# A gated linear recurrence with mixture-of-adapters on one core: inputs laid out on the host by place in the chunk, loads per tile, and a written order

## The chip, the cores and the metric

The kernel runs on one core of a Trainium2 chip. The metric is device time in microseconds (us) of one execution. Before the change, three runs took 126.5, 127.96 and 129.17 us; the median is 127.96.

## What is computed

Four sequences (B = 4) of 768 steps with 8 heads of 48 elements pass through a recurrence with a state of 48 x 48 per head, and the result (3072 tokens of 384 elements) through a mixture of 8 low-rank adapters, of which each token uses two. `x` below is the recurrence's result with the heads side by side, K is 2, and `sel` holds the two logits minus their maximum.

```python
for t in range(S):
    cur = np.einsum('bhd,bhe->bhde', u[None] * kt, vt)
    y[:, :, t] = np.einsum('bhd,bhde->bhe', rt, state + cur)
    state = wt[:, :, :, None] * state + np.einsum('bhd,bhe->bhde', kt, vt)
...
logits = x @ w_gate
topk = np.argpartition(-logits, K, axis=1)[:, :K]
...
w = np.exp(sel)
w /= w.sum(-1, keepdims=True) + 1e-09
...
        z = x[mask] @ A[e]
        delta[mask] += w[mask, k, None] * (z @ B[e])
return x + delta
```

## The kernel before, in words

The tokens are cut into 24 tiles of 128 (six per sequence); a tile's 128 tokens lie on the 128 partitions. Tiles are put into groups (of 1, 2 and 3 tiles in the first sequence, of 3 and 3 in the others) for the logarithm of w (`ln`, L475) and for the conversion of v to bf16 (`vcast`, L481), both on ACT.

For each tile t the work is a fixed set of named tasks:

- Decay: `csr` (PE, L488 to L492) sums the logarithms over the tile with triangular matrices into the bank `cs_ps`; `expr` (ACT, L500) takes the exponential into the bank `e_ps`, and `multr` (DVE, L511) multiplies r by it. `csk`, `expk`, `multk` (L495, L505, L516) do the same for k with the same two banks.
- The term with u: `rkk` and `rku` (POOL, L520 and L524) form r k u, `diag` (DVE, L528) sums it per head, `dv` (POOL, L533) multiplies v by the sum.
- Within the tile: `trr` and `trk` (PE, L540 and L545) transpose both products, `trev` (L551 on DVE in odd tiles, L553 on ACT in even ones) copies them out, `amm` (PE, L562) multiplies them, and `aev` (DVE, L568) copies the product out under the triangular mask, as tile `at`.
- State and output: `kv` (PE, L578) adds to the state, `sev` (ACT, L584) copies it; `yin` and `yat` (PE, L596 to L610) sum the parts of the output, `xTev` (ACT, L616) copies it to `xT`.
- Adapters: `lg` (PE, L621) makes the logits. In gates of 6, 6, 6, 3, 1, 1 and 1 tiles, `lgs` (ACT, L632) copies them, `gmax` (DVE, L640 and L643) finds the two largest, and `gsub`, `gexp`, `gmul`, `gden`, `gnorm` make the weights (on POOL and DVE; from tile 18 on DVE alone). `zmm`, `zw`, `zT`, `zTev` (L697 to L720) form the weighted inner product, `dmm` (PE, L726 and L728) multiplies by B and adds x, `oev` (ACT, L734) copies to `res`, and `store` (L738) is issued from ACT's queue.

Inputs are read as they lie in memory. A load (L390) takes one of w, k, r, v of a whole sequence into a tile whose heads are padded from 48 to 64 elements; each 48 elements of one head and one token are a run of 192 bytes in memory. r of the first sequence is loaded in six pieces by chunk (L392). All loads are issued from SP's queue, in the order of the list `LOADS` (L791), together with u, the gate weights, A and B. A comes in as it lies; PE turns it (`turn_A`, L754) between two ACT copies (L747 and `evac_A`, L759).

Ahead of everything, `consts` (L419 to L433) sets up masks and identities, and DVE clears the padded tiles (L428) and two weight tiles (L432, L433).

The order of the instructions on each engine is decided when the kernel is built: `Plan` simulates the tasks with their costs, dependencies and the priorities in `PRIO`, `PRIO_HEAD` and `PRIO_TAIL`, and emits the tasks in order of their simulated start. Each engine then works through its own instructions in that order, and waits on semaphores where it needs another engine's result.

Of the kernel before, what the change touches and what calls it, by code (L numbers as in the profile page):

```python
# [8 lines left out]
F32 = mybir.dt.float32  # L9
# [12 lines left out]
    aev=25.65,  # L22
    amm=-15.27,
    cast_A=-11.66,
    cast_B=0.88,
    cast_wg=-60.35,
    consts=-10.85,
    csk=-0.31,
    csr=-14.17,
    diag=42.56,  # L30
    dmm=2.74,
    dv=81.69,
    evac_A=-13.75,
    expk=-72.58,
    expr=-39.57,
    gden=-20.59,
    gexp=-17.6,
    gmax=-31.21,
    gmul=-9.69,
    gnorm=-40.58,  # L40
    gsub=-13.25,
    kv=-18.83,
    ld_A=-22.88,
    ld_B=26.38,
    ld_k0=-6.66,
    ld_k1=21.95,
    ld_k2=52.4,
    ld_k3=-5.23,
    ld_r0c0=-4.41,
    ld_r0c1=-34.52,  # L50
    ld_r0c2=-23.64,
    ld_r0c3=-29.83,
    ld_r0c4=1.38,
    ld_r0c5=13.41,
    ld_r1=-3.05,
    ld_r2=17.81,
    ld_r3=52.81,
    ld_u=-83.12,
    ld_v0=-6.77,
    ld_v1=29.59,  # L60
    ld_v2=44.69,
    ld_v3=71.64,
    ld_w0=-43.71,
    ld_w1=13.24,
    ld_w2=41.57,
    ld_w3=24.4,
    ld_wg=-15.62,
    lg=42.53,
    lgs=-10.33,
    ln=21.58,  # L70
    multk=5.22,
    multr=-87.78,
    oev=-1.78,
    rkk=101.18,
    rku=63.0,
    sev=13.54,
    store=-95.56,
    trev=-30.73,
    trk=-25.52,
    trr=-5.99,  # L80
    turn_A=-2.64,
    vcast=110.5,
    xTev=3.03,
    yat=-18.65,
    yin=23.89,
    zT=-24.79,
    zTev=-5.29,
    zmm=26.3,
    zw=-7.91,
# [5 lines left out]
    aev=-16.79,  # L95
    amm=48.01,
    cast_A=7.5,
    cast_B=-14.13,
    cast_wg=21.27,
    consts=-2.5,  # L100
    csk=-21.41,
    csr=-7.4,
    diag=-4.31,
    dmm=17.09,
    dv=38.59,
    evac_A=10.38,
    expk=11.86,
    expr=-16.57,
    gden=-38.35,
    gexp=-14.3,  # L110
    gmax=4.34,
    gmul=-3.71,
    gnorm=-5.33,
    gsub=-43.86,
    kv=12.49,
    ld_A=-5.03,
    ld_B=12.8,
    ld_k0=-34.63,
    ld_k1=6.6,
    ld_k2=-14.77,  # L120
    ld_k3=11.25,
    ld_r0c0=-24.58,
    ld_r0c1=4.07,
    ld_r0c2=15.4,
    ld_r0c3=6.19,
    ld_r0c4=5.17,
    ld_r0c5=-7.65,
    ld_r1=21.36,
    ld_r2=23.52,
    ld_r3=22.62,  # L130
    ld_u=19.76,
    ld_v0=-12.19,
    ld_v1=1.39,
    ld_v2=0.87,
    ld_v3=-20.68,
    ld_w0=8.25,
    ld_w1=-10.57,
    ld_w2=-9.52,
    ld_w3=26.72,
    ld_wg=5.58,  # L140
    lg=4.13,
    lgs=8.09,
    ln=-22.66,
    multk=10.55,
    multr=-21.15,
    oev=14.15,
    rkk=39.57,
    rku=9.98,
    sev=-2.01,
    store=-13.3,  # L150
    trev=22.53,
    trk=31.94,
    trr=6.82,
    turn_A=22.18,
    vcast=-15.78,
    xTev=-6.57,
    yat=-4.27,
    yin=16.18,
    zT=27.26,
    zTev=33.7,  # L160
    zmm=-3.4,
    zw=17.47,
)
PRIO_TAIL = dict(
    aev=-0.28,
    amm=14.03,
    cast_A=-36.85,
    cast_B=19.87,
    cast_wg=11.74,
    consts=-26.49,  # L170
    csk=9.67,
    csr=25.89,
    diag=34.43,
    dmm=6.24,
    dv=-17.71,
    evac_A=8.83,
    expk=-0.72,
    expr=-40.51,
    gden=23.76,
    gexp=18.47,  # L180
    gmax=-30.09,
    gmul=40.84,
    gnorm=18.15,
    gsub=14.82,
    kv=19.73,
    ld_A=-8.96,
    ld_B=-1.13,
    ld_k0=17.68,
    ld_k1=14.83,
    ld_k2=27.67,  # L190
    ld_k3=-8.08,
    ld_r0c0=32.73,
    ld_r0c1=19.97,
    ld_r0c2=-39.7,
    ld_r0c3=29.48,
    ld_r0c4=-20.14,
    ld_r0c5=6.09,
    ld_r1=-4.78,
    ld_r2=-19.27,
    ld_r3=-29.09,  # L200
    ld_u=40.14,
    ld_v0=3.86,
    ld_v1=-4.67,
    ld_v2=-39.21,
    ld_v3=8.49,
    ld_w0=-33.47,
    ld_w1=-3.25,
    ld_w2=39.94,
    ld_w3=6.14,
    ld_wg=8.51,  # L210
    lg=2.86,
    lgs=42.9,
    ln=-1.58,
    multk=19.03,
    multr=21.62,
    oev=-2.62,
    rkk=37.33,
    rku=-39.38,
    sev=4.33,
    store=0.15,  # L220
    trev=-11.58,
    trk=-3.46,
    trr=26.52,
    turn_A=24.22,
    vcast=-21.25,
    xTev=-23.74,
    yat=1.12,
    yin=21.1,
    zT=-2.43,
    zTev=-1.87,  # L230
    zmm=1.73,
    zw=5.22,
)


class Plan:


    HOP = 0.061
    WAIT = 0.047  # L240
# [5 lines left out]
    def add(self, name, eng, cost, base, deps, fn, far=False, take=None, free=None, lat=0.0, dma=0.0):  # L246
        assert name not in self.tasks, name
        op = name if name in PRIO else name.rstrip("0123456789")
        zone = 1 if base < 3 else 2 if base >= 20 else 0
        prio = base + PRIO.get(op, 0.0) + (PRIO_HEAD if zone == 1 else PRIO_TAIL if zone == 2 else {}).get(op, 0.0)  # L250
        self.tasks[name] = dict(name=name, eng=eng, cost=cost, base=base, prio=prio, deps=deps, fn=fn,
                                far=far, take=take, free=free, lat=lat or dict(DVE=.09, ACT=.1, PE=.17, POOL=.05).get(eng, 0.0), dma=dma, i=self.seq, zone=zone)
        self.seq += 1

    def run(self):
        T = self.tasks
        users, left = {n: [] for n in T}, {}
# [11 lines left out]
        def enter(x):  # L269
            e = x["eng"]  # L270
            rdy = 0.0
            for d in x["deps"]:
                rdy = max(rdy, end_of[d] if T[d]["eng"] == e and not x["far"] else done[d] + self.HOP)
            x["rdy"] = rdy
            ready[e].append(x)
# [50 lines left out]
def kernel(  # L326
    ctx: ExitStack,
    tc: tile.TileContext,
    r: bass.AP,
    k: bass.AP,  # L330
    v: bass.AP,
    w: bass.AP,
    u: bass.AP,
    moe_w_gate: bass.AP,
    moe_A: bass.AP,
    moe_B: bass.AP,
# [3 lines left out]
    B, H, S, D = r.shape  # L340
    L = 128
    NC = S // L
    HD = H * D
    NT = B * NC
    P = H // 2
    E = moe_w_gate.shape[1]
    R = moe_A.shape[2]
    ER = E * R
    DP = 64
# [24 lines left out]
    SRC = dict(r=r, k=k, v=v, w=w)  # L374
    seqs = {}

    def seq_tile(b, key):
        d = seqs.setdefault(b, {})
        if key in "rk":
            if "rk" not in d:  # L380
                d["rk"] = ld.tile([L, 2, H * NC, DP], F32, name="rk")
                d["r"], d["k"] = d["rk"][:, 0], d["rk"][:, 1]
        elif key not in d:
            d[key] = ld.tile([L, H * NC, DP], F32, name=key + "_in", bufs=3 if key == "v" else 2)
        return d[key]

    def load(b, key, c):
        dst = seq_tile(b, key)
        if c is None:
            nc.sync.dma_start(out=dst[:, :, 0:D], in_=SRC[key][b].rearrange("h (c p) d -> p (h c) d", p=L))  # L390
        else:
            nc.sync.dma_start(out=dst.rearrange("p (h c) d -> p h c d", c=NC)[:, :, c, 0:D],  # L392
                              in_=SRC[key][b, :, c * L:(c + 1) * L, :].rearrange("h p d -> p h d"))

# [10 lines left out]
    wg_f = const.tile([128, P, E], F32, name="wg_f")  # L405
    A_f = const.tile([E * H, D * R], F32, name="A_f")
    A_nat = const.tile([E * H, DP, R], BF16, name="A_nat")
    B_f = const.tile([ER, HD], F32, name="B_f")
# [10 lines left out]
    def consts():  # L419
# [7 lines left out]
        for t_ in rk2s[:2] + v_bfs[:2] + dvs[:2] + S_sbs + rk2s[2:] + dvs[2:] + v_bfs[2:]:  # L427
            nc.vector.memset(t_, 0.0)  # L428
# [3 lines left out]
        nc.vector.memset(wg_f, 0.0)  # L432
        nc.vector.memset(A_nat, 0.0)  # L433

    def load_u():
        nc.sync.dma_start(out=u_sb, in_=u.partition_broadcast(128))

    def load_wg():
        for g in range(2):
            nc.sync.dma_start(  # L440
                out=wg_f[g * 64:g * 64 + D],
                in_=moe_w_gate.rearrange("(p g d) e -> g d p e", g=2, d=D)[g])

    def load_A():
        nc.sync.dma_start(out=A_f, in_=moe_A.rearrange("e (h d) r -> (e h) (d r)", h=H))

    def load_B():
        nc.sync.dma_start(out=B_f, in_=moe_B.rearrange("e r d -> (e r) d"))  # L448
# [14 lines left out]
    def chunk(t, key):  # L463
        b, c = divmod(t, NC)
        return seqs[b][key].rearrange("p (h c) d -> p h c d", c=NC)[:, :, c, 0:D]

    def chunks(gi, key):
        g = groups[gi]
        x = seqs[g["b"]][key].rearrange("p (h c) d -> p c h d", c=NC)
        return x[:, g["c0"]:g["c0"] + g["n"], :, 0:D]  # L470

    def ln(gi):
        g = groups[gi]
        lw = wk.tile([L, GN, H, D], FP16, name="logw", bufs=3)
        nc.scalar.activation(out=lw[:, 0:g["n"]], in_=chunks(gi, "w"), func=ACT.Ln)  # L475
        g["logw"] = lw
# [158 lines left out]
    def gmax(q):  # L635
# [3 lines left out]
        for i in range(n):  # L639
            nc.vector.max(out=top[:, i, :], in_=x[:, i, :])  # L640
# [300 lines left out]
```

## Time and profile before

| quantity | value |
|---|---|
| median of three runs | 127.96 us (126.5 to 129.17) |
| the profiled execution's own time | 126.82 us |
| its span, first to last instruction | 125.1 us |
| mean granted clock of TensorE | 0.963 |
| bytes read, written | 19.48 MB, 4.72 MB |
| memory clears of padded tiles on DVE, first start to last end | 2.16 to 9.00 us |
| first logarithm (ACT) starts | 13.31 us |
| first and last masked copy `at` (DVE) start | 21.24 and 113.89 us |
| issue to landing, median, of a whole-sequence load of w, k, v | 10.3, 10.4, 11.2 us |
| issue to landing, median, of a store of 192 KB | 1.9 us |

The profile is of one execution. Engines: PE is TensorE's matmuls, PEld its weight loads, DVE is VectorE, ACT ScalarE, POOL GpSimd, SP the engine that issues the loads; SPq and ACTq are those engines' queues, where DMAs are issued. A line such as "L568 DVE" is an instruction of line 568 of the kernel before. The busy rows cut the span into 40 slices, with one digit of tenths for each. A row of the timeline gives start, duration, engine, line, operation, output and inputs with their shapes, how many instructions were merged, and in brackets how long the engine had been idle and what ended that.

### The profile page before, as it was taken

The page shows a single profiled execution, that of the slowest core. Times are in us where ns is not written, and L with a number is a line of the kernel's source. Part 1 is how long each engine was busy: PE and PEld are TensorE (multiplying, and loading weights), DVE is VectorE, ACT ScalarE, POOL GpSimd, SP SyncE. Part 2 cuts the span into 40 slices and gives each one's busy share as a digit, 9 for nine tenths or more (in the row PEclk, how much of TensorE's full clock was granted, in tenths as well). Part 3 has the DMA queues.
Part 4 walks back from the last instruction along what each step waited for, and adds up shares of the span by engine and source line. Part 5 has one row for each costly group of instructions (what it writes and reads, how often), then busy time and mean ns, then how long its engine had stood idle before and what let it go on. Part 6 is the DMA issues. An engine that isn't in the chain of part 4 may idle for free.

```text
span 125.1 us, 3598 instructions
## 1 busy us (share of the span) xinstructions
PE 94.4 (75%) x1432; PEld 66.3 (53%) x1432; DVE 91.9 (73%) x208; ACT 82.6 (66%) x165; POOL 70.6 (56%) x93
## 2 busy tenths in 40 slices
PE   1000399699789496899994599979998999999840
PEld 0000066456557363577673477667675667877520
DVE  5982153576499598999748577977789999989830
ACT  4000783576985468998850979769998886955550
POOL 6000191588493399999379798812069999900000
PEclk9999999999999958999999959999999999999996
DMA  2879996496899799798889959994950321305063
GB/s 49 251 222 291 215 220 190 86 267 168 205 261 284 198 287 291 200 295 218 231 246 277 266 165 259 275 286 122 314 204 0 128 71 63 129 2 189 5 251 126
DMA packets 33776, 24.42 MB, mean 195 GB/s; under 512 B 7328, under 2 KB 33696, under 8 KB 33760
## 3 DMA queue, kind: packets, MB, share of 16 engines
q1 hardware_dynamic: 30304, 19.48, 57.2%
q10 hardware_dynamic: 3456, 4.72, 10.3%
q8 instruction: 11, 0.18, 0.6%
q14 instruction: 5, 0.04, 0.1%
HBM read 19.48 MB, written 4.72 MB: 193 GB/s over the span
## 4 chain that ended last, share of the span: by engine, by line
SPq 36%; DMA 17%; PE 14%; DVE 12%; ACT 9%; issue 5%; POOL 3%; ACTq 1%; DVEq 0%; POOLq 0%
SPq L390 22%; DMA v_in<-in_v_dram 12%; SPq L392 8%; DMA rk<-in_r_dram 5%; DVE at L568 4%; SPq L448 4%; ACT res L734 2%; SPq L440 2%; ACT e_ps L505 2%; DVE rk L511 2%; POOL rku L524 2%; ACT xT L616 2%; POOL rku L520 2%; PE y_ps L596 1%; PE y_ps L610 1%
## 5 line engine op out<-in xcount | busy, mean ns | idle before, releaser
L520 POOL TENSOR_TENSOR rku<-rk 128x384 f32<-128x384 f32 x24 | 24.1, 1004 | 24.7 <-DMA rk<-in_r_dram 21.1
L568 DVE TENSOR_TENSOR at<-a_ps,at_mask 128x1024 bf16<-128x1024 f32 x24 | 29.2, 1217 | 3.3 <-PE a_ps L562 3.1
L533 POOL TENSOR_TENSOR dv<-v_in,diag 128x384 bf16<-128x384 f32 x24 | 19.6, 830 | 10.3 <-DVE diag L528 4.6
L524 POOL TENSOR_TENSOR rku<-rku,u_sb 128x384 f32<-128x384 f32 x24 | 24.0, 999 | 1.6
L511 DVE TENSOR_TENSOR rk<-rk,e_ps 128x384 bf16<-128x384 f32 x24 | 13.1, 547 | 10.5 <-DMA rk<-in_r_dram 7.7
L492 PE MATMUL cs_ps<-logw,strict 128*128 128x384 f16 x24 | 9.0, 374 | 11.9 <-ACT logw L475 11.9
L516 DVE TENSOR_TENSOR rk<-rk,e_ps 128x384 bf16<-128x384 f32 x24 | 13.1, 546 | 5.5 <-ACT e_ps L505 3.8
L475 ACT ACTIVATE logw<-w_in 128x1152 f16<-128x1152 f32 (+2 forms) x9 | 9.4, 1058 | 11.5 <-DMA w_in<-in_w_dram 11.2
L616 ACT CAST xT<-y_ps 128x512 bf16<-128x512 f32 x24 | 14.1, 588 | 3.3 <-PE y_ps L610 3.2
L500 ACT ACTIVATE e_ps<-cs_ps 128x384 f32<-128x384 f32 x24 | 11.5, 478 | 6.8 <-DVE rk L516 3.2
L528 DVE TENSOR_REDUCE diag<-rku 128x8 f32<-128x384 f32 x24 | 12.9, 546 | 2.9 <-POOL rku L524 2.8
L481 ACT CAST v_bf<-v_in 128x1152 bf16<-128x1152 f32 (+2 forms) x9 | 9.3, 1045 | 7.0 <-DMA v_in<-in_v_dram 7.0
L505 ACT ACTIVATE e_ps<-cs_ps 128x384 f32<-128x384 f32 x24 | 11.6, 484 | 3.2 <-PE y_ps L610 1.4
L545 PE MATMUL trp<-ident,rk 128*128 128x128 bf16 x96 | 10.5, 238 | 3.2 <-DVE rk L516 3.2
L734 ACT COPY res<-d_ps 128x384 f32<-128x384 f32 x22 | 10.6, 483 | 2.9 <-PE d_ps L728 1.5
L553 ACT COPY rkT<-trp 128x1024 bf16<-128x1024 bf16 x12 | 12.2, 1014 | 0.4 <-PE trp L545 0.4
L562 PE MATMUL a_ps<-rkT 48*128 48x128 bf16 x192 | 10.2, 229 | 2.2 <-ACT rkT L553 1.3
L540 PE MATMUL trp<-ident,rk 128*128 128x128 bf16 x96 | 10.5, 239 | 1.2 <-ACT rkT L553 0.5
L610 PE MATMUL y_ps<-at,v_bf 128*64 128x128 bf16 x192 | 10.6, 236 | 0.4 <-DVE at L568 0.4
L601 PE MATMUL y_ps<-ident,dv 128*128 128x128 bf16 x96 | 10.0, 229 | 0.0
L551 DVE COPY rkT<-trp 128x1024 bf16<-128x1024 bf16 x12 | 8.2, 684 | 2.1 <-PE trp L545 2.1
L540 PEld LDWEIGHTS <-rk 128*128 128x128 bf16 x96 | 6.9, 106 | 5.1 <-issue 1.9
(74 smaller groups left out, 176.4 us busy)
## 6 DMA issues: line engine op xcount, KB each, us to landing
out_dram<-res ACTq DMA_DIRECT2D x24, 192.0 KB, 1.9
rk<-in_r_dram SPq DMA_DIRECT2D x6, 192.0 KB, 3.5
u_sb<-in_u_dram SPq DMA_DIRECT2D x1, 192.0 KB, 3.7
A_f<-in_moe_A_dram SPq DMA_DIRECT2D x1, 192.0 KB, 4.2
B_f<-in_moe_B_dram SPq DMA_DIRECT2D x1, 192.0 KB, 6.4
rk<-in_k_dram SPq DMA_DIRECT2D x4, 0.2 KB, 10.4
w_in<-in_w_dram SPq DMA_DIRECT2D x4, 0.2 KB, 10.3
v_in<-in_v_dram SPq DMA_DIRECT2D x4, 0.2 KB, 11.2
```

The source lines that it names most:

```text
L390: nc.sync.dma_start(out=dst[:, :, 0:D], in_=SRC[key][b].rearrange("h (c p) d -> p (h c) d", p=L))
L505: nc.scalar.activation(out=e, in_=cs_ps[:, 0:HD].rearrange("p (h d) -> p h d", d=D), func=ACT.Exp, scale=-1.0)
L511: nc.vector.tensor_mul(rk2[:, 0].rearrange("s p h d -> s (p h) d")[:, :, 0:D], chunk(t, "r"), st[t]["er"])
L516: nc.vector.tensor_mul(rk2[:, 1].rearrange("s p h d -> s (p h) d")[:, :, 0:D], chunk(t, "k"), st[t]["ek"])
L520: nc.gpsimd.tensor_mul(rku, chunk(t, "r"), chunk(t, "k"))
L524: nc.gpsimd.tensor_mul(st[t]["rku"], st[t]["rku"], u_sb)
L528: nc.vector.tensor_reduce(out=dg, in_=st[t]["rku"], axis=AX.X, op=ALU.add)
L533: nc.gpsimd.tensor_mul(dv_[:, :, 0:D], chunk(t, "v"), st[t]["diag"].to_broadcast([L, H, D]))
L540: nc.tensor.transpose(trp[:, 0, p, :], st[t]["rk2"][:, 0, p, :, :].rearrange("s a b -> s (a b)"), ident)
L568: nc.vector.tensor_mul(at, st[t]["a_ps"].rearrange("s g p f -> s (g p) f"), at_mask.to_broadcast([128, H, 128]))
L616: nc.scalar.copy(out=xT_, in_=st[t]["y_ps"])
L734: nc.scalar.copy(out=res, in_=st[t]["d_ps"])
```

## The change

The host puts the inputs into the order in which the kernel uses them: partition first, then tile, head, element (`lay_out`), so that each partition reads one run. r and k of one tile stand side by side in one array; u is repeated for all partitions; the gate weights, A (already turned and padded) and B are one array of 128 rows.

- Loads: one for w and one for v of each group (9 each), one for r and k of each tile (24), one for u, one for the adapter weights: 44, all from SP, into tiles without pad. Buffers: 3 for w, 4 for v, 8 for r and k; `logw` has 4 instead of 3.
- The constants: only the pad columns of the padded work tiles are cleared, and `turn_A`, `evac_A` and the two clears of weight tiles are gone. The three casts read the one weight tile.
- Stores are issued from SP instead of ACT, in the same queue as the loads.
- Gates: the selection `gsel` becomes a task apart from `gmax`. Where a gate has one tile (21, 22, 23), `gnorm` is gone: `zw` multiplies by the weights and by the reciprocal at once. From tile 18 the logits are read from PSUM without `lgs`.
- For tiles 18 to 23, `dx` adds x into the result bank ahead of `dmm`, which then is a single matmul.
- The order is a list of all tasks, `ORDER`, instead of the planner's result. The planner's code is changed too but not used.

Core of the diff:

```diff
+ORDER = """
+consts ld_w0 ld_rk0 ln0 csr0 ld_v0 expr0 rkk0 ld_w1 csk0 multr0 vcast0 expk0 trr0 ld_u multk0 ln1 ld_rk1 kv0 rku0
+csr1 trk0 sev0 expr1 ld_rk2 rkk1 trev0 csk1 multr1 diag0 ld_v1 expk1 amm0 csr2 trr1 multk1 rku1 dv0 rkk2 trk1 aev0
+ld_w2 expr2 vcast1 yin0 csk2 multr2 trev1 rku2 expk2 kv1 yat0 ld_rk3 ln2 diag1 amm1 trr2 csr3 diag2 multk2 dv1
...
+ln3 ld_rk7 rkk6 amm4 diag5 multk5 yat3 cast_A csr6 ld_rk8 aev4 xTev3 lg0 trk5 expr6 yin4 rku6 rkk7 dv5 cast_B ld_v3
...
+expk13 ld_w7 vcast6 csr14 multk13 yat11 zTev3 diag15 expr14 amm12 multr14 store2 ld_rk18 dmm3 trk13 csk14 xTev11
...
+xTev14 expk17 sev16 aev15 trev16 ld_v8 lg14 yin15 csr18 multk17 yat15 amm16 rku19 rku20 zTev6 expr18 diag18 dmm6
+xTev15 multr18 store0 oev6 aev16 csk18 trr17 trk17 expk18 rkk21 rku21 dv18 yin16 store1 ld_rk23 vcast8 trev17 csr19
...
+gden5 zmm22 zT21 dmm19 oev18 zmm23 gexp6 zw22 gsel6 zTev21 dx20 oev19 dmm20 gmul6 store18 gden6 zT22 oev20 dx21 zw23
+dmm21 store19 zTev22 zT23 dx22 oev21 dmm22 zTev23 store20 dx23 dmm23 oev22 store21 oev23 store22 store23
+"""
...
-            nc.sync.dma_start(out=dst[:, :, 0:D], in_=SRC[key][b].rearrange("h (c p) d -> p (h c) d", p=L))
...
+    def load_w(gi):
+        g = groups[gi]
+        g["w"] = ld.tile([L, GN, H, D], F32, name="w_in", bufs=3)
+        nc.sync.dma_start(out=g["w"][:, 0:g["n"]], in_=w[:, g["t0"]:g["t0"] + g["n"]])
+
+    def load_v(gi):
+        g = groups[gi]
+        g["v"] = ld.tile([L, GN, H, D], F32, name="v_in", bufs=4)
+        nc.sync.dma_start(out=g["v"][:, 0:g["n"]], in_=v[:, g["t0"]:g["t0"] + g["n"]])
+
+    def load_rk(t):
+        st[t]["rk"] = ld.tile([L, 2, H, D], F32, name="rk_in", bufs=NRKI)
+        nc.sync.dma_start(out=st[t]["rk"], in_=rk[:, t])
...
-        for t_ in rk2s[:2] + v_bfs[:2] + dvs[:2] + S_sbs + rk2s[2:] + dvs[2:] + v_bfs[2:]:
-            nc.vector.memset(t_, 0.0)
+        pads = [t_.rearrange("s a p h d -> s (a p h) d") for t_ in rk2s]
+        pads += [t_.rearrange("s c h d -> s (c h) d") for t_ in v_bfs] + dvs + S_sbs
+        for t_ in pads:
+            nc.vector.memset(t_[:, :, D:DP], 0.0)
...
+        if alone(q):
+            nc.vector.scalar_tensor_tensor(
+                out=zw_[:, 0], in0=st[t0]["z_ps"][:, 0].rearrange("p (e r) -> p e r", r=R),
+                scalar=gst[q]["den"][:, 0, :], in1=gst[q]["gs"].rearrange("p o e -> p e o").to_broadcast([L, E, R]),
+                op0=ALU.mult, op1=ALU.mult)
+            return
...
-    def dmm(t):
+    def dx(t):
         d_ps = bank(dbank(t), [L, HD], F32, "d_ps")
-        nc.tensor.matmul(d_ps, lhsT=st[t]["zT"], rhs=B_bf, start=True, stop=False, skip_group_check=True)
         for p in range(P):
             nc.tensor.matmul(d_ps[:, p * 2 * D:(p + 1) * 2 * D], lhsT=st[t]["xT"][:, p, :], rhs=ipad,
-                             start=False, stop=(p == P - 1), skip_group_check=True)
+                             start=(p == 0), stop=False, skip_group_check=True)
         st[t]["d_ps"] = d_ps
+
+    def dmm(t):
+        if not own_bank(t):
+            dx(t)
+        nc.tensor.matmul(st[t]["d_ps"], lhsT=st[t]["zT"], rhs=B_bf, start=False, stop=True, skip_group_check=True)
...
-        nc.scalar.dma_start(out=out[t * 128:(t + 1) * 128, :], in_=st[t]["res"])
+        nc.sync.dma_start(out=out[t * 128:(t + 1) * 128, :], in_=st[t]["res"])
...
-    NXT, NRES = 12, 8
+    NXT, NRES, NRKI = 12, 8, 8
...
+    def tok(x):
+        return x.reshape(B, H, S // L, L, D).transpose(3, 0, 2, 1, 4).reshape(L, B * S // L, H, D)
...
+    return dict(
+        w=tok(w), rk=np.stack([tok(r), tok(k)], axis=2), v=tok(v), u=np.broadcast_to(u, (L, H, D)),
+        moe=np.concatenate([rows(moe_w_gate), rows(moe_A.transpose(1, 0, 2).reshape(H * D, E * R)),
+                            moe_B.reshape(E * R, H * D)], axis=1))
```

## The prediction

> **What bounds the kernel now.** I read the page's busy shares and slices first, then the DMA queues, the waits, and the windows and timeline of single stages.
>
> ```profile
> PE 94.4 (75%) x1432; PEld 66.3 (53%) x1432; DVE 91.9 (73%) x208; ACT 82.6 (66%) x165; POOL 70.6 (56%) x93
> PE   1000399699789496899994599979998999999840
> ...
> DMA  2879996496899799798889959994950321305063
> ...
> q1 hardware_dynamic: 30304, 19.48, 57.2%
> q10 hardware_dynamic: 3456, 4.72, 10.3%
> ...
> SPq 36%; DMA 17%; PE 14%; DVE 12%; ACT 9%; issue 5%; POOL 3%; ACTq 1%; DVEq 0%; POOLq 0%
> ```
>
> No engine is full over the span. The slices show two stages: the DMA engines are about nine tenths busy up to slice 29 (91 us), while PE is full only from there. The chain is 36% SP queue and 17% DMA: loads set the pace. Loads (q1) used 0.572 x 16 x 125.1 = 1145 engine-us for 19.48 MB, 58.8 per MB; stores (q10), rows of 1536 B, 206 for 4.72 MB, 43.7 per MB.
>
> ```profile
> POOL rku L520 <- DMA rk<-in_r_dram: 21.1, 5, 12.3
> ACT logw L475 <- DMA w_in<-in_w_dram: 11.2, 1, 11.2
> DVE rk L511 <- DMA rk<-in_r_dram: 7.7, 3, 5.0
> ACT v_bf L481 <- DMA v_in<-in_v_dram: 7.0, 3, 3.4
> ```
>
> These waits (total, count, longest) show the first w arriving 11.2 us after ACT was ready, and later sequences starving the engines again.
>
> ```profile
> 13.31 1.26 ACT L475 ACTIVATE logw<-w_in 128x384 f16<-128x384 f32 x2 [11.24 <-DMA w_in<-in_w_dram]
> 15.12 0.56 DVE L511 TENSOR_TENSOR rk<-rk,e_ps 128x384 bf16<-128x384 f32 x1 [4.99 <-DMA rk<-in_r_dram]
> 21.24 1.23 DVE L568 TENSOR_TENSOR at<-a_ps,at_mask 128x1024 bf16<-128x1024 f32 x1 [1.38 <-PE a_ps L562]
> 96.64 1.22 DVE L568 TENSOR_TENSOR at<-a_ps,at_mask 128x1024 bf16<-128x1024 f32 x1
> 113.89 1.22 DVE L568 TENSOR_TENSOR at<-a_ps,at_mask 128x1024 bf16<-128x1024 f32 x1
> 91.00:114.00 23.00, 22.26 (x386) 16.52 (x384) 22.06 (x55) 18.18 (x43) 17.19 (x21) 1.00 0.23 85
> ```
>
> Each tile has one masked copy of `at` (L568), so its start marks the tile. The first is at 21.24, the last (tile 23) at 113.89: 92.65 / 23 = 4.03 us per tile. From tile 18 (96.64) to 23, with all loads landed, it is 17.25 / 5 = 3.45. The window row gives busy time of PE, PEld, DVE, ACT, POOL: PE 22.26 and DVE 22.06 of 23 us, so compute bounds there. The end after the last `at` is 125.1 - 113.89 = 11.2. Three parts then: head 21.2, 23 intervals, tail 11.2.
>
> **Head.** Loads become one run per partition of 1536 to 4608 B, and w of tile 0 alone comes first, 192 KB. Landing, issue to data: 1.9 us for a 192 KB store, 3.7 for the 192 KB u load with others beside it. Issue at 0.8 gives 2.7 to 4.5; I take 3.4, between the two and nearer the store, since w is first in the queue. From the start of the log (13.31) to the end of the first exponential (14.48 + 0.47) is 1.64, so multr could start at 5.1. Its r and k (384 KB) are next: at 43.7 to 58.8 engine-us per MB (2.7 to 3.7 us per MB on 16 engines) they land 1.1 to 1.5 us after w, in time.
>
> DVE's own start also counts: it clears padded tiles until 10.1. Now only the pad columns are cleared. A memset of 512 words took 485 ns, of 128 words 165: 0.83 ns per word and 58 fixed. The 15 pad memsets cost 2.2 us if done in words, 3.6 if in 2-byte elements, against 6.2 before; wg_f and A_nat (0.57) go. DVE starts these at 2.16 and is free at 5.3 to 6.7; I take 6.0 for multr of tile 0.
>
> Multr to `at` took 21.24 - 15.12 = 6.1. Of that amm waited 1.5 for the A transposition on PE (2.11 us) and the work queued behind it, which the host now does: 4.6 is left (multr 0.56, expk 0.47, multk 0.56, trk 0.63, trev 1.0, amm 0.65, hops). First `at`: 10.6 (9.9 to 11.3). cast_A with its 512 elements costs what evac_A did (0.59 of ACT), later, beside PE's work.
>
> **Middle.** Bytes per tile: 19.48 / 24 = 0.81 MB, 2.2 us at the stores' price, 3.0 at the old loads' price. Both are under 3.45, so after the head DMA should run ahead, up to the eight rk buffers. In list order 3.54 MB stand up to rk of tile 3; at the old price of 3.7 us per MB it lands at 2.8 + 13.0 = 15.8, and its multr wants it at 6.0 + 3 x 3.45 = 16.4: little slack there, a microsecond or two of risk.
>
> The per-tile price has ends 3.3 (100 to 110 us, where PE ran 181 of its 1432 matmuls, 3.03 tiles) and 4.03 (the whole of before, starved). I take 3.6: 3.45, nearest because its loads were there, plus 0.15 for clock dips: twice in the middle the granted clock falls to 0.5 for 3.4 us, 2 x 1.7 / 23. 23 x 3.6 = 82.8.
>
> One rule bears on the dips: the Trainium skill, TensorE: Matmul & The Clock Gate, Part 1, says that the clock is halved after an idle window of about 3.4 us and released by activity. The first dip follows PE waits of 0.65 and 1.03 us at 41 to 43, when loads were late, so the trace does not show a whole idle window. By the rule a fed PE would have no dip, and the sum would be 3.4 lower.
>
> Other edits here: the 24 stores leave ACT (0.34 each, 8.2 us of its issue time, mostly under running ACT work) and go to SP behind loads. SP issues 44 loads and 24 stores. At 0.39 (u) to 0.82 (the first k) that is 27 to 56 us of queue time, beside compute, against issues blocked for 4 to 6 us each now. Store 0 is put behind the loads of v8; its buffer is wanted by oev8 only, eight tiles later, so I price it at nothing; if the cover fails, oev8 waits, and dmm9 behind it for the bank. Reads without pad cost nothing new: POOL took 1004 ns with pad (L520), 999 without (L524). The order list replaces the planner's; no row shows its quality, and 3.3 to 4.03 bounds it.
>
> A rule that speaks against the change: the Trainium skill, DMA: Bandwidth & Descriptors, Rules for kernel authors, asks for 1 MiB or more per DMA for full bandwidth; these are 0.19 to 0.58 MB. Its anatomy of the GpSimd path puts some 2.0 us of fixed cost on each, and if 44 loads paid that in series, my estimate from that page is 88 us of latency and no gain. The last stores show otherwise: they are issued 0.95 us apart while each takes 1.9 to land, so they overlap.
>
> **Tail.** The last rows of ACT are copies of `res` 0.95 apart, 0.48 of work and 0.47 behind a store's issue.
>
> ```profile
> 120.78 0.48 ACT L734 COPY res<-d_ps 128x384 f32<-128x384 f32 x1 [0.47 <-ACT res L734]
> 121.29 0.34 ACTq L738 DMA_DIRECT2D out_dram<-res  x1
> 121.72 0.48 ACT L734 COPY res<-d_ps 128x384 f32<-128x384 f32 x1 [0.47 <-ACT res L734]
> ```
>
> With stores on SP the last copy follows its own matmul (ends 120.9) instead of ACT's queue: -0.7. The last gate loses the normalisation (0.27 from 119.20 to 119.47) and the logit copy (0.17 and a hop), though the fused product may cost up to 0.17 more than the 0.28 of the plain one: -0.4. dx ahead of time takes 0.33 of matmul off the last result: -0.3. 11.2 - 1.4 = 9.8; bounds 9.3 and 11.2.
>
> **Sum.** 10.6 + 82.8 + 9.8 = 103.2 of span. The profiled execution took 126.82 for a span of 125.1, 1.7 around it: 104.9, say 105. That execution lies 0.9% under the median shown, 127.96; I leave 105.
>
> **Rivals.** *Loads still pace it.* If runs of a few KB gain nothing, or waits in SP's list make loads late, the rate stays 4.03: 10.6 + 92.7 + 9.8 + 1.7 = 114.8. For: DMA was nine tenths busy; against: 43.7 against 58.8 per MB, and prefetch eight tiles deep. *Better than fed before.* The list packs all engines at 3.3 and DVE is free early: 9.9 + 75.9 + 9.3 + 1.7 = 96.8. Against: in 91 to 114 PE had 0.7 us idle, little to win. *Slower than before.* SP works strictly in order, so a load whose buffer is late holds all loads behind it; place: ld_rk9 on, each waiting for tile t-8. Price: were each tile's landing of 1.9 us bare, 105 + 23 x 1.9 = 148.7. It decides from 1.0 us bare per tile (128 - 105 = 23). Against: ld_rk8 stands in the list beside tile 4's work, four tiles ahead. *No change*, 125 to 130, needs the same loss at about 1.0 per tile; nothing speaks for it.
>
> **How the numbers follow.** Forecast 0.69; loads pacing 0.15; better 0.08; slower 0.05; no change 0.03. Faster by over 2% (about what a measurement of this kernel can tell from no change) takes the first three: 0.92; within 2%: 0.03; slower: 0.05. The range reaches from the better case, 97, to the pacing case, 115; beyond it lie the 0.08 and some of both ends.
>
> **What would show it.** First log near 3.4, first multr near 6, first `at` near 10.6; `at` spacing 3.4 to 3.7 with PE nine tenths busy; no wait on rk or w above 2 us after the head; queue 1 near 44 engine-us per MB; last `at` near 93.4 and 9.8 after it. Wrong if `at` spacing is near 4 with POOL or DVE waiting on rk, if PE's clock stays at 0.5 for long, or if engines wait on each other in turn with DMA idle: then the list is at fault.

## The result and the profile after

The kernel after takes 103.27 us (median of four runs, 102.98 to 103.59), against 127.23 for the kernel before on the same chip. The ratio is 0.820, with a 95% interval of 0.812 to 0.829. Ratios, here and below, leave out executions more than 1.5% slower than the fastest of the same kernel, so they are not quite the quotients of the medians. The profiled execution took 103.02 us for a span of 101.3. The forecast was 105 with a range of 97 to 115.

The page of the kernel after, in the rows that were shown of before (busy shares; tenths in 40 slices for PE and the DMA engines; the DMA queue; the chain that ended last, by engine):

```profile
PE 85.6 (84%) x1400; PEld 60.7 (60%) x1400; DVE 85.2 (84%) x203; ACT 80.5 (79%) x160; POOL 69.8 (69%) x93
PE   1238899998698699999999999999988999999930
...
DMA  2899999999999976948006989961224003224173
...
q1 hardware_dynamic: 9792, 24.27, 64.5%
...
PE 54%; DVE 22%; ACT 7%; DMA 5%; issue 4%; POOL 3%; SPq 1%; ACTq 1%; DVEq 0%
```

From slice 4 on, PE is now at eight tenths or more in nearly every slice; before, it kept falling to four to seven tenths up to slice 27. The SP queue has gone from the chain, 36% to 1%, and DMA from 17% to 5%. DMA is full or nearly so from slice 2 to slice 14 (35 us), while it runs ahead of the engines, and then has gaps: it no longer sets the pace. Loads and stores now stand in one queue, 0.645 x 16 x 101.3 = 1045 engine-us for 24.27 MB, 43.1 per MB; before it was 58.8 for the loads.

The waits of the kernel after that end on a load (total, count, longest):

```profile
POOL rku L422 <- DMA u_sb<-in_u_dram: 2.6, 1, 2.6
...
POOL rku L418 <- DMA rk_in<-in_rk_dram: 1.7, 1, 1.7
...
ACT v_bf L379 <- DMA v_in<-in_v_dram: 1.6, 1, 1.6
...
ACT logw L373 <- DMA w_in<-in_w_dram: 1.2, 1, 1.2
```

Each occurs once, and all in the first 8.2 us. The first logarithm waits 1.2 us instead of 11.2. From there on no engine waits for a load.

The timeline of the kernel after, its head and the first and last masked copy (start, duration, engine, line):

```profile
3.27 0.52 ACT L373 ACTIVATE logw<-w_in 128x384 f16<-128x384 f32 x1 [1.19 <-DMA w_in<-in_w_dram]
4.87 0.55 DVE L409 TENSOR_TENSOR rk<-rk_in,e_ps 128x384 bf16<-128x384 f32 x1 [0.51 <-ACT e_ps L398]
6.40 0.51 ACT L379 CAST v_bf<-v_in 128x384 bf16<-128x384 f32 x1 [1.56 <-DMA v_in<-in_v_dram]
6.82 0.47 ACT L403 ACTIVATE e_ps<-cs_ps 128x384 f32<-128x384 f32 x1
9.56 1.01 ACT L451 COPY rkT<-trp 128x1024 bf16<-128x1024 bf16 x1
11.46 1.22 DVE L466 TENSOR_TENSOR at<-a_ps,at_mask 128x1024 bf16<-128x1024 f32 x1
91.06 1.22 DVE L466 TENSOR_TENSOR at<-a_ps,at_mask 128x1024 bf16<-128x1024 f32 x1
```

In three parts, profiled execution against profiled execution:

| part | before | after | forecast |
|---|---|---|---|
| head, to the first `at` | 21.24 | 11.46 | 10.6 |
| middle, 23 intervals | 92.65 (4.03 each) | 79.60 (3.46 each) | 82.8 (3.60 each) |
| tail, after the last `at` starts | 11.2 | 10.24 | 9.8 |
| span | 125.1 | 101.3 | 103.2 |

More than half of the gain, 13.0 us, comes from the middle, 9.8 from the head, 1.0 from the tail.

### The profile page after: what moved, and what is told of

The parts are those of the page before. It is cut to its first block, busy times and chain, and to the rows that moved or that the text cites. A ratio compares the mean times of both kernels' runs of the same rounds, so it can differ in the third digit from the quotient of the medians.

```text
span 101.3 us, 3568 instructions
## 1 busy us (share of the span) xinstructions
PE 85.6 (84%) x1400; PEld 60.7 (60%) x1400; DVE 85.2 (84%) x203; ACT 80.5 (79%) x160; POOL 69.8 (69%) x93
## 3 DMA queue, kind: packets, MB, share of 16 engines
q1 hardware_dynamic: 9792, 24.27, 64.5%
HBM read 19.55 MB, written 4.72 MB: 240 GB/s over the span
## 4 chain that ended last, share of the span: by engine, by line
PE 54%; DVE 22%; ACT 7%; DMA 5%; issue 4%; POOL 3%; SPq 1%; ACTq 1%; DVEq 0%
DVE at L466 8%; PE y_ps L508 6%; PE a_ps L460 6%; PE y_ps L499 5%; PE y_ps L494 5%; DMA v_in<-in_v_dram 5%; PE trp L438 4%; PE z_ps L601 4%; PE d_ps L640 4%; PE trp L443 3%; DVE rk L414 3%; DVE rkT L449 3%; PE s_ps L476 3%; PE cs_ps L388 3%; PE s_ps L519 3%
## 5 line engine op out<-in xcount | busy, mean ns | idle before, releaser
L418 POOL TENSOR_TENSOR rku<-rk_in 128x384 f32<-128x384 f32 x24 | 23.9, 998 | 1.7 <-DMA rk_in<-in_rk_dram 1.7
L409 DVE TENSOR_TENSOR rk<-rk_in,e_ps 128x384 bf16<-128x384 f32 x24 | 13.2, 548 | 2.9 <-ACT e_ps L398 2.9
L414 DVE TENSOR_TENSOR rk<-rk_in,e_ps 128x384 bf16<-128x384 f32 x24 | 13.2, 549 | 2.6 <-ACT e_ps L403 2.5
L651 ACT COPY res<-d_ps 128x384 f32<-128x384 f32 x22 | 10.6, 486 | 2.6 <-PE d_ps L647 2.1
L438 PE MATMUL trp<-ident,rk 128*128 128x128 bf16 x96 | 9.8, 227 | 1.0 <-DVE rkT L449 0.7
L390 PE MATMUL cs_ps<-logw,strict 128*128 128x384 f16 x24 | 8.4, 349 | 2.1 <-ACT logw L373 2.1
L508 PE MATMUL y_ps<-at,v_bf 128*64 128x128 bf16 x192 | 9.8, 224 | 0.2
L443 PE MATMUL trp<-ident,rk 128*128 128x128 bf16 x96 | 9.8, 227 | 0.1
L393 PE MATMUL cs_ps<-logw,ident 128*128 128x384 f16 x24 | 8.3, 348 | 0.7 <-ACT e_ps L398 0.6
```

The source lines that it names most:

```text
L409: nc.vector.tensor_mul(rk2[:, 0].rearrange("s p h d -> s (p h) d")[:, :, 0:D], chunk(t, "r"), st[t]["er"])
L414: nc.vector.tensor_mul(rk2[:, 1].rearrange("s p h d -> s (p h) d")[:, :, 0:D], chunk(t, "k"), st[t]["ek"])
L418: nc.gpsimd.tensor_mul(rku, chunk(t, "r"), chunk(t, "k"))
L438: nc.tensor.transpose(trp[:, 0, p, :], st[t]["rk2"][:, 0, p, :, :].rearrange("s a b -> s (a b)"), ident)
L443: nc.tensor.transpose(st[t]["trp"][:, 1, p, :], st[t]["rk2"][:, 1, p, :, :].rearrange("s a b -> s (a b)"), ident)
L508: nc.tensor.matmul(y_ps[g * 64:(g + 1) * 64, p, :], lhsT=vb[:, 2 * p + g, :], rhs=at[:, g * P + p, :], start=False, stop=(p == P - 1), ski ...
```

## The experiments

All times are medians. The ratio is to the kernel before, measured together with each kernel; its medians lay between 125.9 and 128.7. The kernels came in three groups on three chips (runs of 192 bytes, whole sequences, planner, full clears; then stores from ACT and less work on PE, DVE, POOL; then the rest), and the kernel after was not measured again with them, so I read nothing into differences below 0.7 us from it. Parts such as head, spacing and tail are read from one profiled execution of each kernel. Theory at the outset: the loads had set the pace; long runs made them cheap, an early small first load brought the first tile forward, and what is left is bound by compute, PE first.

**Run length alone undone.**

```diff
-        nc.sync.dma_start(out=st[t]["rk"], in_=rk[:, t])
+        nc.sync.dma_start(out=st[t]["rk"].rearrange("p x h d -> p (x h) d"), in_=rk[t].rearrange("x h p d -> p (x h) d"))
...
-        return x.reshape(B, H, S // L, L, D).transpose(3, 0, 2, 1, 4).reshape(L, B * S // L, H, D)
+        return x.reshape(B, H, S // L, L, D).transpose(0, 2, 1, 3, 4).reshape(B * S // L, H, L, D)
...
```

(w and v in the same way.)

> Undoes the run length alone: the host still lays inputs out by tile, in the order of use, but head by head, so that each load reads runs of 192 bytes; loads, buffers and order stay. Theory (the gain is the early first tile and the loads' order; the middle is bound by compute at 3.45 us per tile): loads cost 58.8 engine-us per MB again, which is 3.0 us per tile and still under 3.45, so 104 to 108, first at masked copy at 12 to 13. Rival (the run length itself is what fed the engines): loads pace the middle as before, 4.0 us per tile, 114 or more.

Measured: 133.23 us, ratio 1.036 (1.031 to 1.041): slower than the kernel before. The theory's number fell, and the rival's 4.0 us per tile was not far enough out. The page, two waits and three masked copies (the first, the seventh, the last) of this kernel:

```profile
DMA packets 102737, 24.50 MB, mean 186 GB/s; under 512 B 99392, under 2 KB 102592, under 8 KB 102720
...
q1 hardware_dynamic: 102720, 24.27, 90.7%
```

```profile
POOL rku L418 <- DMA rk_in<-in_rk_dram: 25.2, 10, 4.3
ACT v_bf L379 <- DMA v_in<-in_v_dram: 16.0, 8, 4.9
```

```profile
12.53 1.22 DVE L466 TENSOR_TENSOR at<-a_ps,at_mask 128x1024 bf16<-128x1024 f32 x1
42.55 1.22 DVE L466 TENSOR_TENSOR at<-a_ps,at_mask 128x1024 bf16<-128x1024 f32 x1 [0.26 <-PE a_ps L460]
120.95 1.21 DVE L466 TENSOR_TENSOR at<-a_ps,at_mask 128x1024 bf16<-128x1024 f32 x1
```

The head is nearly that of the kernel after (12.5 against 11.5), but the spacing is (120.95 - 12.53) / 23 = 4.71, and POOL waits ten times for r and k. The reason is the first line. The kernel before read the same runs of 192 bytes, but its page counts 33,776 packets in all, 7,328 of them under 512 B; here there are 102,737, of which 99,392 are under 512 B. A load of a whole sequence went out mostly in packets between 512 B and 2 KB, a load of one to three tiles in packets of one run each; what makes the difference was not isolated. So the old price did not come back, a worse one did: 0.907 x 16 x 131.6 = 1910 engine-us; without the stores (206 in the kernel before) an estimated 1704 for 19.55 MB, 87 per MB. That is 4.4 us per tile, more than the 3.46 of compute. Small loads need the long runs.

**Load size alone undone.** The long runs stay, but each of w, v and r with k comes for a whole sequence.

```diff
-        nc.sync.dma_start(out=st[t]["rk"], in_=rk[:, t])
+        if t % NC == 0:
+            whole["rk"] = ld.tile([L, NC, 2, H, D], F32, name="rk_in", bufs=2)
+            nc.sync.dma_start(out=whole["rk"], in_=rk[:, t:t + NC])
+        st[t]["rk"] = whole["rk"][:, t % NC]
...
```

> Undoes the size alone: long runs as after, but w, v and r with k are each loaded for a whole sequence (1.1 and 2.3 MB) where the list has the first piece. Theory (the first tile waits for its bytes): w lands near 6, r and k near 12.5, so the first multr at 13 instead of 4.9; the middle keeps 3.45; about 110. Rival (large DMAs move faster, and the size of a load costs nothing): 102 to 104.

Measured: 112.22 us, ratio 0.872 (0.867 to 0.877). The theory holds in the main (about 110 was expected), and so do its parts:

```profile
19.40 1.22 DVE L476 TENSOR_TENSOR at<-a_ps,at_mask 128x1024 bf16<-128x1024 f32 x1
98.97 1.22 DVE L476 TENSOR_TENSOR at<-a_ps,at_mask 128x1024 bf16<-128x1024 f32 x1
```

The first log starts at 6.04 and the first multr at 11.65 (6 and 13 expected); ACT then waits for v until 14.34, which the theory had left out. The first `at` is 7.9 us later than in the kernel after, the spacing is the same 3.46, and the end is 8.3 later. Large loads are not faster either: from 3 to 25 us this kernel moved 427 GB/s, the kernel after 415 from 10 to 30, both with all DMA engines full.

**The list taken away.**

```diff
-ORDER = """
-consts ld_w0 ld_rk0 ln0 csr0 ld_v0 expr0 rkk0 ld_w1 csk0 multr0 vcast0 expk0 trr0 ld_u multk0 ln1 ld_rk1 kv0 rku0
...
-"""
+ORDER = ""
```

> Takes the list away: the planner orders the tasks by its costs and the priorities of the kernel after; loads keep their order. Theory (feeding the engines is the change; any sane order gives 3.45): 102 to 106. Rival (the list holds a good part of the gain): 108 or more.

Measured: 160.23 us; its executions spread from 153 to 161, so no ratio is given. The theory falls: an order is not just any order. The first `at` comes at 9.46, earlier than in the list, but the spacing is 5.15, and 30.9 us follow the last `at` instead of 10.2. DMA is idle for most of the second half, so this is not a load. POOL waits 18.9 us for `diag`, ACT 17.9 for PE's outputs. From 115 us on the granted clock is 0.54 on average, so a part of the loss is PE at half speed. It shows that order can cost over 50 us with the same work and loads, but not what the list is worth against the order of the kernel before, since the planner ran here with other costs and priorities.

**The layout alone, in the kernel before.** This gives the missing corner: long runs, whole-sequence loads, the old planner's order, clears and store queue.

```diff
-            nc.sync.dma_start(out=dst[:, :, 0:D], in_=SRC[key][b].rearrange("h (c p) d -> p (h c) d", p=L))
+            nc.sync.dma_start(out=dst, in_=SRC[key][b].rearrange("p c h d -> p (c h) d"))
...
+        inputs[name] = x.reshape(x.shape[0], x.shape[1], -1, 128, x.shape[3]).transpose(0, 3, 2, 1, 4)
```

> Makes the layout alone in the kernel before: r, k, v, w by place in the chunk, tiles without pad, so that whole-sequence loads are one run per partition and the pieces of r 1536 bytes each; number, size and order of the loads, the planner, stores from ACT and clears stay. Theory (the run length fed the engines, the rest is the head): spacing 3.4 to 3.6 instead of 4.03, first masked copy 14 to 17, 107 to 113. Rival (the old order, which the planner made for slow loads, keeps the engines apart when fed): 116 or more.

Measured: 116.63 us (115.77 to 118.73), ratio 0.938 (0.916 to 0.960): at the edge of the rival's range, and outside the theory's. The profiled execution took 117.49:

```profile
19.45 1.22 DVE L565 TENSOR_TENSOR at<-a_ps,at_mask 128x1024 bf16<-128x1024 f32 x1 [1.28 <-PE a_ps L559]
104.54 1.22 DVE L565 TENSOR_TENSOR at<-a_ps,at_mask 128x1024 bf16<-128x1024 f32 x1
```

Read beside the whole-sequence kernel, this splits the gain in three, by profiled executions. Layout alone, 126.82 to 117.49: the spacing goes from 4.03 to (104.54 - 19.45) / 23 = 3.70 (3.4 to 3.6 expected), and the head only from 21.2 to 19.5 (14 to 17 expected), since whole sequences still come first. The list with all the other edits (clears, queue of the stores, adapter weights, gates), 117.49 to 111.39: the head stays (19.45, 19.40), the spacing goes to 3.46. Small loads, 111.39 to 103.02: the spacing stays, the head goes to 11.5. That is 9.3, 6.1 and 8.4 us. The first two are good to some 2 us only, as two executions of this kernel took 115.77; and the 6.1 is not the list's alone.

**Clears of whole tiles.**

```diff
-            nc.vector.memset(t_[:, :, D:DP], 0.0)
+            nc.vector.memset(t_, 0.0)
```

> Undoes the short clears alone: DVE clears whole tiles again, 6.2 us instead of 1.9. Theory (DVE's start is on the path of the first tile once the data is early): DVE free near 8.6, first multr 8.7 instead of 4.9, time 2.5 to 4 us longer, 105.8 to 107.3. Rival (hidden, since expk of tile 0 waits for other work until 6.8 anyway, and lookahead takes the rest): 103 to 104.

Measured: 107.54 us, ratio 0.837 (0.833 to 0.842). The theory holds: 4.3 us longer, a little over its range. DVE's first multr starts at 10.08 instead of 4.87 (8.7 expected), with no wait ahead of it:

```profile
10.08 0.55 DVE L409 TENSOR_TENSOR rk<-rk_in,e_ps 128x384 bf16<-128x384 f32 x1
```

The first `at` starts at 15.36 instead of 11.46, and the spacing is 3.48. A delay of 3.9 in the head is a delay of about 4 at the end.

**Stores from ACT.**

```diff
-        nc.sync.dma_start(out=out[t * 128:(t + 1) * 128, :], in_=st[t]["res"])
+        nc.scalar.dma_start(out=out[t * 128:(t + 1) * 128, :], in_=st[t]["res"])
```

> Undoes the queue of the stores alone: issued from ACT again, at the same places of the list. Theory (prediction): only the tail pays, where copies of res stand 0.95 us apart behind store issues: 0.7 longer, 103.8 to 104.3. Rival (ACT, 80% busy, pays for 24 issues of 0.34 in the middle too): 106 or more. Rival: no difference, since the last result comes late by its own chain.

Measured: 103.96 us (103.57 to 104.71), 0.7 over the kernel after, which was measured on another chip. The size is the theory's, and the end is where it shows: in the profiled execution the last six intervals take 22.61 us against 22.22, the tail 10.45 against 10.24. Its spacing is 3.52 against 3.46 for another reason, too: from 28.2 to 31.6 us the granted clock was 0.5, which the profiled execution of the kernel after does not have. From the 10th to the 18th `at`, with the clock at 1.0 in both, it takes 24.86 us against 24.87, so the middle pays nothing. With a difference this small, between chips, I still count the size as unproven.

**Work taken from PE, DVE, POOL and ACT.** Four kernels ask which engine bounds the middle. Each leaves out work of one engine.

```diff
-        d_ps = bank(dbank(t), [L, HD], F32, "d_ps")
-        for p in range(P):
-            nc.tensor.matmul(d_ps[:, p * 2 * D:(p + 1) * 2 * D], lhsT=st[t]["xT"][:, p, :], rhs=ipad,
-                             start=(p == 0), stop=False, skip_group_check=True)
-        st[t]["d_ps"] = d_ps
+        st[t]["d_ps"] = bank(dbank(t), [L, HD], F32, "d_ps")
...
-        nc.tensor.matmul(st[t]["d_ps"], lhsT=st[t]["zT"], rhs=B_bf, start=False, stop=True, skip_group_check=True)
+        nc.tensor.matmul(st[t]["d_ps"], lhsT=st[t]["zT"], rhs=B_bf, start=True, stop=True, skip_group_check=True)
```

> Leaves out the addition of x to the result (96 of 1400 matmuls, 0.17 us per tile of PE, 4.1 us in all). Theory (PE bounds from 40 us on): 3 to 4 us shorter, about 99.5 to 100.5. Rival (DVE bounds, or the chains between engines): under 1 us shorter.

Measured: 102.23 us, 1.0 shorter than the kernel after, and 1.1 and 1.3 shorter than the next two kernels, which were measured together with it.

```diff
-        nc.vector.tensor_reduce(out=dg, in_=st[t]["rku"], axis=AX.X, op=ALU.add)
+        nc.vector.tensor_reduce(out=dg, in_=st[t]["rku"][:, :, 0:8], axis=AX.X, op=ALU.add)
```

> Leaves out most of one sum on DVE: diag adds 8 of 48 elements per head (0.33 us per tile less, 7.9 us in all). Theory (PE bounds): under 1.5 us shorter. Rival (DVE bounds, which was also 85% busy): 5 to 8 us shorter.

Measured: 103.33 us, no difference.

```diff
-        nc.gpsimd.tensor_mul(st[t]["rku"], st[t]["rku"], u_sb)
+        nc.gpsimd.tensor_mul(st[t]["rku"][:, :, 0:8], st[t]["rku"][:, :, 0:8], u_sb[:, :, 0:8])
```

> Leaves out most of one product on POOL: u multiplies 8 of 48 elements per head (about 0.7 us per tile less, 17 us in all). Theory (PE bounds; POOL runs ahead and ends its work at 80): under 1 us shorter. Rival (POOL, nearly full from 10 to 72, paces the first two thirds): 3 us shorter or more.

Measured: 103.48 us, no difference.

```diff
-        nc.scalar.copy(out=vb[:, 0:g["n"], :, 0:D], in_=g["v"][:, 0:g["n"]])
+        lo = {4: 1, 5: 2}.get(gi, 0)
+        if gi < 6:
+            nc.scalar.copy(out=vb[:, lo:g["n"], :, 0:D], in_=g["v"][:, lo:g["n"]])
```

> Leaves out 4.3 us of ACT's work in the middle: the casts of v of the last three groups and parts of two others, whose products then use older values. Theory (no single engine): under 1 us shorter, 102.3 or more. Rival (ACT, 92% busy from 10 to 70, is the bound that the three other cuts missed): 3 us shorter or more, 100 or less.

Measured: 103.44 us, no difference. So no single engine is the bound of the whole; less work on PE gains 1.0 us of the 4.1 left out, less on the others nothing. The last of these kernels leaves out at once what the first three left out.

> Leaves out, all at once, what three kernels left out one by one: the addition of x on PE, most of the sum on DVE, most of the product with u on POOL. Theory (several engines are near full, and each single cut only met the next one): more than the sum of the three single gains, 3 us shorter or more, 100 or less. Rival (the steps of a tile that pass between ACT, DVE and PE through single banks set 3.46 us, whatever the engines' load): 101.5 to 103.

Measured: 100.77 us, ratio 0.812 (0.802 to 0.821): 2.5 shorter than the kernel after, between the two numbers. Where it is shorter decides. The window rows from 10 to 70 us (busy PE, PEld, DVE, ACT, POOL, with the number of instructions; then the granted clock, the DMA share and GB/s), of the kernel after, of the one with less on PE, and of the one with less on all three, the last one from 10 to 40 us as well:

```profile
10.00:70.00 60.00, 55.47 (x936) 39.48 (x936) 56.85 (x109) 55.08 (x107) 57.71 (x69) 1.00 0.82 307
```

```profile
10.00:70.00 60.00, 55.30 (x897) 38.54 (x897) 56.64 (x108) 54.82 (x107) 57.41 (x68) 1.00 0.83 309
```

```profile
10.00:40.00 30.00, 26.87 (x413) 18.62 (x414) 24.07 (x52) 26.07 (x50) 21.56 (x34) 0.94 0.95 373
10.00:70.00 60.00, 55.58 (x901) 38.98 (x901) 51.28 (x109) 54.89 (x107) 43.67 (x68) 0.97 0.82 305
```

The 10th and the 18th `at` of the kernel after and of the one with less on all three:

```profile
43.97 1.22 DVE L466 TENSOR_TENSOR at<-a_ps,at_mask 128x1024 bf16<-128x1024 f32 x1
68.84 1.22 DVE L466 TENSOR_TENSOR at<-a_ps,at_mask 128x1024 bf16<-128x1024 f32 x1
```

```profile
44.37 1.22 DVE L466 TENSOR_TENSOR at<-a_ps,at_mask 128x1024 bf16<-128x1024 f32 x1
68.62 1.22 DVE L466 TENSOR_TENSOR at<-a_ps,at_mask 128x1024 bf16<-128x1024 f32 x1
```

POOL lost 14 us of 57.7 and DVE 5.6 of 56.9, and ACT still issued the same 107 instructions. From the first to the 18th `at` the spacing is (68.84 - 11.46) / 17 = 3.375 after and (68.62 - 11.36) / 17 = 3.368 with less on all three. But the two are not alike: this profiled execution is the slowest of five (101.46 us), and its granted clock fell to 0.5 from 28.1 to 31.5 us. From the 6th to the 8th `at`, across this dip, it took 8.51 us, and the kernels with less on POOL and with stores from ACT, which had the same dip, 8.55; the kernel after took 7.70. So the dip costs about 0.8. From the 10th to the 18th `at`, with the clock at 1.0 in all of them, the kernels compare without it: 24.87 us after, 24.86 with less on PE, 24.54 on DVE, 24.87 on POOL, 24.87 on ACT, 24.25 on the first three at once. At the end, from the 18th to the 24th `at`, it is 22.2 us after, 21.2 with less on all three and 21.0 with less on PE alone, and the tail is 0.2 to 0.3 shorter. So of the 2.5 us about 1.3 are gained at the end, and about 1 in the first two thirds (0.6 measured, the rest an estimate with the dip's 0.8).

Neither number held. In the first two thirds a quarter of POOL's work and a tenth of DVE's are worth about 1 us of 57, so their load does not set the pace there, nor does ACT's. PE's load was tried there only lightly: 39 of its 936 matmuls were left out, without a gain. In the last third PE's load counts. That the steps which pass from engine to engine in the written order set the pace of the first two thirds, as the rival has it, is what is left; it is argued, not shown, and which chain of steps sets 3.4 us was not isolated. The chain that ended last in the kernel after lies on PE for 54% and on DVE for 22% of the span. A candidate is the one `e_ps` bank, which each tile uses four times in turn (two exponentials on ACT, two products on DVE), each queued behind instructions of 1.2 us of the same engine; this too is argued only.

The rows also show why PE looked like the bound: with 39 fewer matmuls its busy time is the same, 55.30 against 55.47, while its weight loads fell from 39.48 to 38.54. The Trainium skill, Trainium Kernel Development and Optimization, Performance Expectations, calls matmul busy time a bad metric, since matmuls are pipelined; this case agrees.

**The head's order.**

```diff
-consts ld_w0 ld_rk0 ln0 csr0 ld_v0 expr0 rkk0 ld_w1 csk0 multr0 vcast0 expk0 trr0 ld_u multk0 ln1 ld_rk1 kv0 rku0
-csr1 trk0 sev0 expr1 ld_rk2 rkk1 trev0 csk1 multr1 diag0 ld_v1 expk1 amm0 csr2 trr1 multk1 rku1 dv0 rkk2 trk1 aev0
+consts ld_w0 ld_rk0 ln0 csr0 ld_v0 expr0 rkk0 ld_w1 csk0 multr0 expk0 trr0 ld_u multk0 vcast0 trk0 ln1 ld_rk1 rku0
+trev0 csr1 kv0 expr1 sev0 ld_rk2 rkk1 csk1 multr1 diag0 ld_v1 expk1 amm0 csr2 trr1 multk1 rku1 dv0 rkk2 trk1 aev0
```

> Changes the list for tile 0 alone: the cast of v goes behind the second exponential of tile 0, the transposition of k and its copy go ahead of tile 0's state and tile 1's decay. Theory (what the head loses passes to the end one for one, as the full clears and the whole-sequence loads showed, each with the same spacing): the second exponential starts at 5.5 instead of 6.8, the first masked copy at 9 to 9.5 instead of 11.5, time 1.5 to 2.5 shorter, 100.8 to 101.8. Rival (tile 1 is held by its own data, w at 7.4 and u at 8.1, so only tile 0 moves): 102.7 to 103.5.

Measured: 102.84 us, ratio 0.829 (0.822 to 0.836); 0.4 under the kernel after, which was measured on another chip, so a gain is not shown. The second exponential did start at 5.88 instead of 6.82:

```profile
5.88 0.47 ACT L403 ACTIVATE e_ps<-cs_ps 128x384 f32<-128x384 f32 x1 [0.92 <-DVE rk L409]
6.26 0.50 ACT L379 CAST v_bf<-v_in 128x384 bf16<-128x384 f32 x1
7.21 0.84 ACT L373 ACTIVATE logw<-w_in 128x768 f16<-128x768 f32 x1 [0.44 <-DMA w_in<-in_w_dram]
7.96 0.99 ACT L451 COPY rkT<-trp 128x1024 bf16<-128x1024 bf16 x1
```

But the copy of the transposed products then stands behind the logarithm of tile 1, whose w lands at 7.2, and the product after it on PE behind tile 1's decay: the first `at` is at 10.99 instead of 11.46. This follows the rival, though `amm0` was not moved forward in the list, so the theory was tried in half only.

## Why the prediction was right, point by point

- *Loads set the pace before, and long runs take that away.* Right. The price per MB was forecast at 43.7 from the stores' rows and came out at 43.1, no wait on a load is left after 8.2 us, and undoing the runs alone loses everything. Long runs alone were not enough, though: in the kernel before they brought the spacing to 3.70, and the rest of the way to 3.46 came with the list and the other edits.
- *First log at 3.4, first multr at 6.0.* 3.27 and 4.87. The clears are done in words and cost less than the 2.2 of the lower bound: 0.59 + 0.84 + 0.33 + 0.17 = 1.9 us in the trace. DVE was free at 4.35, not at 5.3 to 6.7, and waited for the exponential. The 5.3 was also added up wrongly: a start at 2.16, clears of 2.2 and the 0.5 of small copies that follow them before (8.97 to 9.46) make 4.9.
- *4.6 from multr to `at`.* Mis-sized: 6.6. I took the chain's rows and did not read what the list puts between them. It places vcast0 ahead of expk0, so ACT waited for v until 6.40, and tile 0's transposition of k behind tile 1's decay. With both moved, the 6.6 became 5.8 (5.22 to 10.99), so they are not all of it. The first `at` came at 11.46, just over the bound of 11.3; the multr that came 1.1 early hid a part of the error.
- *3.6 us per tile: 3.45 and 0.15 for clock dips.* 3.46. The 0.15 did not come: in the profiled execution of the kernel after the granted clock was 1.0 in every stage up to the last microseconds. The rule of the clock gate (the Trainium skill, TensorE: Matmul & The Clock Gate, Part 1), by which, as I read it, a fed PE has no dip, was right for this term: 23 x 3.45 is 79.4, measured 79.6. Its sum, 3.4 lower than mine, is 101.5; the profiled execution took 103.02, so as a whole it missed by 1.5, mine by 1.9. Nor is a fed PE safe: three kernels that differ little from this one (stores from ACT, less on POOL, less on all three) show one dip each in their profiled executions. That page's table puts a whole idle window ahead of a dip; in the kernel before PE was busy for 1.91 and 1.45 of the 3.40 us ahead of the two dips, and in these three for 2.37 of 3.40.
- *Compute bounds there.* The number stood, the reading of it did not. PE and DVE were nearly full in the fed stretch of the kernel before, but less work on one engine moved the time by 1.0 us or less in all four trials. That 3.45 came back as a mean of 3.46 is partly luck: the first 17 intervals are 3.375, and the last five, the very tiles on which 3.45 had been read, are (91.06 - 72.36) / 5 = 3.74. No engine alone sets it; the order of the steps is part of it, as the planner's 5.15 shows. The prediction had bounded what the list could do by 3.3 to 4.03, and an order can be far outside that.
- *Tail 9.8.* 10.24. Stores from ACT would cost some 0.7, as forecast, over the last six tiles and the tail.
- *The sum.* Head and tail came out 0.9 and 0.4 longer than forecast, the middle 3.2 shorter, so the total was nearer than its largest part.
- *Full bandwidth asks for large DMAs* (the rule that spoke against the change; the Trainium skill, DMA: Bandwidth & Descriptors, Rules for kernel authors): whole-sequence loads moved 427 GB/s, loads of 0.2 to 0.6 MB 415, so the runs show a loss of 3% at most here.
- *Rivals.* "Loads still pace it" was priced at 114.8 with the old price per MB. With the runs left short the time was 133.23, slower than before: small loads of short runs cost 87 per MB, which no row of the kernel before showed. "Slower than before" named the wrong mechanism, SP held up by a late buffer: no engine waits for a load after 8.2 us. The two ways to a slower kernel that the runs did show, small loads of short runs and a bad order, it did not name.

## What to carry to other kernels

Read the price per byte of each queue, and split a load into small pieces only when each piece still has long runs: here 0.2 to 0.6 MB in runs of 1.5 to 4.6 KB moved as fast as 2.3 MB, while the same pieces in runs of 192 bytes lost everything. Load first a piece just large enough for the first tile, and keep other work off that tile's path: what the head lost, to whole-sequence loads (7.9 us) or to full clears (3.9), showed at the end nearly one for one (8.3 and 4.3). Read the clock of two profiled executions before comparing their stages. An engine that is 95% busy is not yet the bound: take work off it and see, before costing an edit by its busy time. A number that comes out right as a mean can still be wrong in each stage.

## What the runs showed of the hardware that was not expected

- The same 192-byte runs went out in packets mostly of 512 B to 2 KB when one load took a whole sequence of a tensor, and in packets of one run when a load took one to three tiles: 33,776 packets against 102,737 for 24.4 and 24.5 MB in all.
- One core's loads moved 414 to 428 GB/s in many of the slices of the kernel after, and up to 447 in the whole-sequence kernel.
- The granted clock fell to half for 3.4 us after stretches of 3.4 us in which PE was busy 43 and 56% of the time (the kernel before) or 70% (2.37 us, in the kernels with stores from ACT, with less on POOL and with less on all three). The kernel after has the same 2.37 us of PE in that stretch, from 24.8 to 28.2 us, and no dip, so PE's load alone does not decide it.
- In the planner's order, which left PE waiting on other engines, the mean granted clock was 0.79.
